# Nystrom attention with a gated MLP on one core: buffers at multiples of 64 bytes, one visit for W and its turned form, a shorter inverse root, another order in the first chunk

## The chip, the cores and the metric

One core of a Trainium2 chip runs the whole program. The metric is the device time of one execution in microseconds; it was measured three times before the change, and one more execution was profiled.

## What is computed

```python
def _attn_ref(q, k, v):                       # 8 batches, 8 heads, 576 tokens, 64 wide
    m = 32                                    # landmarks: means over 18 tokens
    scale = 1.0 / np.sqrt(D)
    ...
    A = sm(q, k_lm)                           # softmax of scaled products
    Bm = sm(q_lm, k_lm)
    C = sm(q_lm, k)
    Z = Bm.transpose(0, 1, 3, 2) / (norm1(Bm) * norminf(Bm) + 1e-06)
    for _ in range(6):
        Z = 2 * Z - Z @ Bm @ Z
    return (A @ Z @ C @ v).astype(np.float32)

def _moe_ref(x, w_gate, w_val, w_out, rms_g): # 4608 tokens of 512, d_ff 1536
    rms = np.sqrt(np.mean(x * x, axis=-1, keepdims=True) + 1e-06)
    xn = x / rms * rms_g
    g = xn @ w_gate
    silu = g * (1.0 / (1.0 + np.exp(-g)))
    val = xn @ w_val
    return (silu * val @ w_out).astype(np.float32)
```

The heads of the attention are joined to rows of 512, and these are the tokens of the MLP.

## The kernel before

**Stages of a batch.** `sums` makes the landmark sums lmT (DVE). `front` computes the products sC, sA and psB on PE, their maxima mx on DVE and the exponentials E on ACT; `turn` and `values` turn E and form C v (sE, ET, pCV); `soften` makes A. The inverse is a Newton iteration on PV: `newton_start`, six `newton_step`s (PE makes pn, DVE makes the next PV, the last one VF = 2 PV - pn). Then `newton_weights` multiplies with Bs into pW and copies it as W, and `newton_values` turns W on PE (pT) and multiplies with the gain gsb into WT. `second` computes the attention output pO from W and AT, its squares sq, their sums pss and pms, the inverse root of ms in r1 by operations on 18 columns (DVE), and an, AT scaled by the root, as a high part (ACT) and a low part (DVE).

**The MLP.** `mix_weights` multiplies WT with the gate and value weights of a pair of feature blocks, wgv, into pM, and splits it into Mhi and Mlo. So psg and psv come straight from an: per block and half of the tokens, 6 matmuls of 288 columns each for gate and value, in fp32r. SiLU is on ACT (s), the product with psv on DVE, and h holds the result's high and low part. Then pso sums h times the out weights (whio, wloo) over 6 blocks, 3 matmuls of 512 columns each, h stationary and the weights moving. d_ff is done in two halves: phase 1 goes over all batches with the first 6 blocks, phase 2 over all batches with the last 6 (lgv, lhio, lloo), and adds phase 1's sums. A chunk is one batch in one phase.

**Weights.** They are decoded from the bits read: two operations on ACT (L175, L178), two on DVE (L180, L183) for each quarter of a wgv, in the order of the class `Weights`.

**Order.** `Mixer` fills the MLP's matmuls with parts of later batches: each part is a generator that waits until a given number of matmuls of a chunk has been issued (`until`). For the first chunk these numbers are in the list `at` of `steady`, for the others in `enter` and `after`. `issue_after` holds an instruction behind another in the order. Each engine takes its instructions in the order of the program.

**Layout.** gsb takes 32 bytes of a partition, and with that the buffers allocated behind it (weights wgv, whio, wloo, an, s, h, Mhi, Mlo, qk, and lgv6 to lhio6 and lloo6) begin 32 bytes past a multiple of 64. lhio7 to lhio11 and lloo7 to lloo11, and the small pools on the other side, begin at multiples of 64.

## Time and profile before

| | |
|---|---|
| median of 3 runs | 837.14 us (836.75 to 837.6) |
| profiled execution | 836.84 us |
| its span in the trace | 834.7 us |
| PE busy | 800.4 us, 96% of the span |
| DVE, ACT, POOL busy | 490.9, 350.9, 71.0 us |
| chain that ended last | PE 86%, DVE 5%, DMA 4%, ACT 2% |
| PE in that chain | pso 35%, psg 19%, psv 18%, pM 6% |

The profiled execution is 0.3 us below the median, and 2.1 us of it lie around the span. A row of a timeline gives the start in us from the span's start, the duration, the engine, the line, and what is written from what. Matmul records overlap: the time of one in a row is the distance of two starts. An fp32 matmul stands as two records, an fp32r one as one.

### The profile page before, as it was taken

The page shows a single profiled execution, that of the slowest core. Times are in us where ns is not written, and L with a number is a line of the kernel's source. Part 1 is how long each engine was busy: PE and PEld are TensorE (multiplying, and loading weights), DVE is VectorE, ACT ScalarE, POOL GpSimd, SP SyncE. Part 2 cuts the span into 40 slices and gives each one's busy share as a digit, 9 for nine tenths or more (in the row PEclk, how much of TensorE's full clock was granted, in tenths as well). Part 3 has the DMA queues.
Part 4 walks back from the last instruction along what each step waited for, and adds up shares of the span by engine and source line. Part 5 has one row for each costly group of instructions (what it writes and reads, how often), then busy time and mean ns, then how long its engine had stood idle before and what let it go on. Part 6 is the DMA issues. An engine that isn't in the chain of part 4 may idle for free.

```text
span 834.7 us, 17401 instructions
## 1 busy us (share of the span) xinstructions
PE 800.4 (96%) x7192; PEld 630.3 (76%) x7192; DVE 490.9 (59%) x1095; ACT 350.9 (42%) x749; POOL 71.0 (9%) x97
## 2 busy tenths in 40 slices
PE   7756999999999999999999999999999999999998
PEld 4334667877878778777787879797979797979796
DVE  7787976856768748668584945242524252425241
ACT  4557644535445444445464844141414141414140
POOL 1012411020020200201110110000000000000000
PEclk8579999999999999999999999999999999999999
DMA  9756452250440612503436510413141304130202
GB/s 326 242 172 216 143 191 89 84 195 15 144 136 2 228 65 92 188 2 109 140 114 229 176 71 13 145 54 118 22 146 53 121 22 147 50 124 14 88 14 75
DMA packets 41054, 95.49 MB, mean 114 GB/s; under 512 B 4112, under 2 KB 17424, under 8 KB 38928
## 3 DMA queue, kind: packets, MB, share of 16 engines
q1 hardware_dynamic: 40976, 94.39, 33.4%
q8 instruction: 56, 0.92, 0.5%
q14 instruction: 22, 0.18, 0.1%
HBM read 66.06 MB, written 28.31 MB: 113 GB/s over the span
## 4 chain that ended last, share of the span: by engine, by line
PE 86%; DVE 5%; DMA 4%; ACT 2%; POOL 1%; issue 1%; SPq 1%; ACTq 0%; DVEq 0%
PE pso L109 35%; PE psg L109 19%; PE psv L109 18%; PE pM L109 6%; PE pn L109 2%; DMA wrawg<-in_moe_w_gate_dram 2%; PE pO L109 1%; PE sC L109 1%; PE pss L109 1%; DMA wrawv<-in_moe_w_val_dram 1%; PE pCV L109 1%; DMA qk<-in_k_dram 1%; PE sE L112 1%; DVE wgv L180 1%; SPq L152 0%
## 5 line engine op out<-in xcount | busy, mean ns | idle before, releaser
L109 PE MATMUL pso<-whio,h 128*128 128x512 f32 x432 | 140.7, 397 | 2.1 <-ACT ob L848 2.1
L109 PE MATMUL pso<-lhio,h 128*128 128x512 f32 x432 | 138.7, 396 | 0.0
L316 DVE TENSOR_TENSOR s<-s,psv 128x288 f32<-128x288 f32 x192 | 85.9, 450 | 60.0 <-PE psv L109 59.3
L315 ACT ACTIVATE s<-psg 128x288 f32<-128x288 f32 x192 | 78.7, 410 | 89.9 <-PE psg L109 89.5
L268 ACT CAST Mhi<-pM 128x512 fp32r<-128x512 f32 x96 | 51.4, 591 | 137.6 <-PE pM L109 137.2
L323 ACT CAST h<-s 128x576 fp32r<-128x576 f32 x96 | 64.6, 673 | 86.2 <-DVE s L316 86.2
L109 PEld LDWEIGHTS pso<-whio,h 128*128 128x128 f32 x432 | 81.6, 189 | 24.3 <-issue 4.2
L109 PEld LDWEIGHTS pso<-lhio,h 128*128 128x128 f32 x432 | 81.0, 187 | 24.8 <-DVE obl L911 5.9
L324 DVE TENSOR_TENSOR h<-s,h 128x576 fp32r<-128x576 f32 x96 | 72.7, 758 | 44.5 <-ACT h L323 44.3
L109 PE MATMUL psg<-an,Mhi 128*128 128x288 f32 x384 | 85.4, 307 | 4.8 <-ACT s L315 3.4
L911 DVE TENSOR_TENSOR obl<-obl,pso 128x512 f32<-128x512 f32 x36 | 24.8, 688 | 107.6 <-PE pso L109 107.4
L109 PE MATMUL pso<-wloo,h 128*128 128x512 f32 x216 | 86.4, 400 | 0.0
L109 PE MATMUL pso<-lloo,h 128*128 128x512 f32 x216 | 85.2, 395 | 0.0
L109 PE MATMUL psv<-an,Mhi 128*128 128x288 f32 x384 | 84.4, 303 | 0.0
L270 DVE TENSOR_TENSOR Mlo<-pM,Mhi 128x512 fp32r<-128x512 f32 x94 | 60.3, 683 | 37.5 <-ACT Mhi L268 37.5
L109 PE MATMUL psg<-anl,Mhi 128*128 128x288 f32 x384 | 81.7, 301 | 0.6 <-DVE Mlo L270 0.6
L109 PE MATMUL psv<-anl,Mhi 128*128 128x288 f32 x384 | 79.1, 294 | 0.0
L109 PEld LDWEIGHTS psg<-an,Mhi 128*128 128x128 f32 x384 | 62.3, 191 | 17.5 <-issue 6.7
L109 PEld LDWEIGHTS psg<-anl,Mhi 128*128 128x128 f32 x384 | 60.9, 188 | 15.5 <-issue 12.6
L109 PEld LDWEIGHTS psv<-an,Mhi 128*128 128x128 f32 x384 | 61.6, 188 | 6.1 <-issue 2.2
L109 PEld LDWEIGHTS psv<-anl,Mhi 128*128 128x128 f32 x384 | 61.5, 188 | 0.0
L109 PE MATMUL psg<-an,Mlo 128*128 128x288 f32 x192 | 58.5, 305 | 0.0
(138 smaller groups left out, 1249.8 us busy)
## 6 DMA issues: line engine op xcount, KB each, us to landing
qk<-in_q_dram SPq DMA_DIRECT2D x16, 576.0 KB, 4.8
qk<-in_k_dram SPq DMA_DIRECT2D x16, 576.0 KB, 5.8
ad<-an SPq DMA_DIRECT2D x8, 1152.0 KB, 5.1
pd<-ob SPq DMA_DIRECT2D x36, 256.0 KB, 2.4
anl<-ad SPq DMA_DIRECT2D x8, 1152.0 KB, 5.1
obl<-pd SPq DMA_DIRECT2D x36, 256.0 KB, 2.7
out_dram<-obl SPq DMA_DIRECT2D x36, 256.0 KB, 2.0
vt<-in_v_dram SPq DMA_DIRECT2D x16, 512.0 KB, 4.1
```

The costliest lines, as they stand in the source:

```text
L109: tc.keep_in_program_order(nc.tensor.matmul(*args, **kw))
L112: tc.keep_in_program_order(nc.tensor.transpose(*args))
L180: nc.vector.scalar_tensor_tensor(w, w, 3, wtail, op0=ALU.logical_shift_left, op1=ALU.bitwise_or)
L268: nc.scalar.copy(hi[:, g], ps[g])
L270: nc.vector.tensor_sub(lo[:, g], ps[g], hi[:, g].bitcast(F32))
L315: silu["last"] = nc.scalar.activation(s[:, cols], banks[0], AF.Silu).ins
L316: nc.vector.tensor_mul(s[:, cols], s[:, cols], banks[1])
L323: nc.scalar.copy(h[:, 0, TAIL:], s)
L324: gated[b, f0 // NF1, 2 * n + i] = nc.vector.tensor_sub(h[:, 1, TAIL:], s, h[:, 0, TAIL:].bitcast(F32))
L911: nc.vector.tensor_add(ob, ob, ps)
```

## The change

It has four parts. First, gsb is padded to 64 bytes and a new buffer `blocks` takes 1024, so that all the buffers named under Layout begin at multiples of 64. Second, `blocks` holds the four matrices Bs of a batch as a block diagonal (written by four POOL copies per batch); two matmuls with it give W's content and two more give it turned, both in one bank, so that the transposes of W and the copy between go, and the two functions become one; VF is written twice side by side for it. Third, the inverse root takes 8 operations on DVE where it took 10. Fourth, in the first chunk `sums(1, 0)` and `front(1, 0)` go between the parts of `second(0)`, ahead of the first `mix_weights`; the fifth quarter of the weights is decoded earlier; `sums(1, 1)` goes behind the decode of the second pair; the mix for the first chunk's next pair is taken one half later; and the positions of the later parts are other numbers (in the last list, that of the later batches, by one or a few).

```diff
     ones = cst.tile([P, M], F32, name="ones")
     nc.vector.memset(ones, 1.0)
-    gsb = cst.tile([P, NK], F32, name="gsb")
+    gsb = cst.tile([P, 16], F32, name="gsb")[:, :NK]
     WT = cst.tile([P, B, NK, 2 * M], F32, name="WT")
+    blocks = cst.tile([P, 2, P], F32, name="blocks")
+    nc.gpsimd.memset(blocks, 0.0)
...
-                if very and i and n + 1 < NPAIR:
-                    mix_weights(wts, b, pairs[n + 1])
-                    yield 1.1
                 s = mp.tile([P, S], F32, name="s", tag="s", bufs=2)
                 for e in range(2):
+                    if very and i and e and n + 1 < NPAIR:
+                        mix_weights(wts, b, pairs[n + 1])
+                        yield 1.1
                     cols = slice(e * HS, (e + 1) * HS)
                     banks = []
...
             if b:
-                tail(after)
+                tail(late or after)
...
             with tc.high_priority():
-                newton_weights(b, inverse[2])
-            yield 0.4, 0.0
-            yield from until(*next(at))
-            with tc.high_priority():
-                newton_values(b)
-            yield 0.3, 0.0
+                newton_weights(b)
+            yield 0.6, 0.0
             stage["newton"] = stage["wt"] = b
...
-            yield 0.0, TW
-            new_state(1)
-            sums(1, 0)
             while stage["second"] < 0:
                 yield -0.3
-            front(1, 0, fixed["an", 0].ins)
-            load_qk(2, 0)
-            yield 1.3, 0.0
-            sums(1, 1, fixed["mx", 1, 0].ins)
-            yield from until(0, 24)
+            yield from until(0, 12)
             turn(1, 0)
             yield 0.65, 0.0
-            yield from until(0, 36)
+            yield from until(0, 37)
+            sums(1, 1, early.last)
+            yield from until(0, 46)
             front(1, 1)
             load_qk(2, 1)
             yield 1.3, 0.0
             inverse = newton_start(1)
-            at = [46, 58, 70] + [78 + 8 * n for n in range(6)] + [126, 132, 138, n_gv + 4, n_gv + 10, n_gv + 18]
+            at = [54, 66, 78] + [84 + 7 * n for n in range(6)] + [126, 136, n_gv + 4, n_gv + 10, n_gv + 18]
             yield from rest(1, inverse, [(0, n) for n in at])
             for b in range(2, B):
...
-                after = [7 * n for n in range(7)] + [48, 54, 68, 86, 96]
+                after = [7 * n for n in range(6)] + [48, 56, 68, 86, 96]
                 yield from rest(b, inverse, [(c, n) for n in enter[3:]] + [(c + 1, n) for n in after])
...
+            Bs = sm.tile([P, 2, M], F32, name="Bs", tag="Bs", bufs=1)
             nc.vector.tensor_mul(Bs, Bm, den.unsqueeze(2).broadcast_to([P, 2, M]))
-            return BT, den, Bs
-
-        def newton_first(b, BT, den, Bs):
+            for h in range(4):
+                nc.gpsimd.tensor_copy(blocks[rows(h), :, rows(h ^ 1)], Bs[rows(h)])
+            return BT, den
+
+        def newton_first(b, BT, den):
             p0 = bmm(BT, BT, M, "p0")
...
                 pn = bmm(PV[:, :, :M], PV[:, :, M:], D, "pn")
-                nt["VF"] = to = sm.tile([P, 2, D], F32, name="VF", tag="VF", bufs=1)
-                of = PV[:, :, M:]
+                nt["VF"] = sm.tile([P, 2, 2, D], F32, name="VF", tag="VF", bufs=1)
+                for g in range(2):
+                    of, by = (a[:, g].unsqueeze(1).broadcast_to([P, 2, D]) for a in (PV[:, :, M:], pn))
+                    nc.vector.scalar_tensor_tensor(nt["VF"][:, g], of, 2.0, by, op0=ALU.mult, op1=ALU.subtract)
+                return
             nc.vector.scalar_tensor_tensor(to, of, 2.0, pn, op0=ALU.mult, op1=ALU.subtract)
 
-        def newton_weights(b, Bs):
+        def newton_weights(b):
+
             VF = state[b]["VF"]
-            pW = pa.tile([P, 2, D], F32, name="pW", tag="pa")
-            for g in range(2):
-                for h in range(4):
-                    r = rows(rho(g, h))
-                    mm(pW[rows(pos(g, h)), g], Bs[r, g, :], VF[r, g, :], start=True, stop=True)
-            W = sm.tile([P, 2, 2, D], F32, name="W", tag="W", bufs=2)
-            fixed[b] = nc.vector.tensor_copy(W, pW.unsqueeze(2).broadcast_to([P, 2, 2, D]))
+            pW = pa.tile([P, 2 * D + NK * 2 * M], F32, name="pW", tag="pa")
+            straight = pW[:, : 2 * D].rearrange("p (g d) -> p g d", g=2)
+            turned = pW[:, 2 * D :].rearrange("p (g n) -> p g n", g=2)
+            for g in range(2):
+                mm(straight[:, g], blocks[:, g], VF[:, g, 0], start=True, stop=True)
+            for g in range(2):
+                mm(turned[:, g], VF[:, g].rearrange("p a d -> p (a d)"), blocks[:, g], start=True, stop=True)
+            W = sm.tile([P, 2, D], F32, name="W", tag="W", bufs=2)
+            fixed[b] = nc.vector.tensor_copy(W, straight)
+            fixed["WT", b] = nc.vector.tensor_mul(
+                WT[:, b],
+                turned.rearrange("p g (j n) -> p (g j) n", j=2),
+                gsb.unsqueeze(2).broadcast_to([P, NK, 2 * M]),
+            )
             state[b]["W"] = W
-
-        def newton_values(b):
-            W = state[b]["W"]
-            pT = pa.tile([P, NK, 2 * M], F32, name="pT", tag="pa")
-            for g in range(2):
-                tp(
-                    pT[:, 2 * g : 2 * g + 2].rearrange("p j n -> p (j n)"),
-                    W[:, g].rearrange("p a d -> p (a d)"),
-                    ident,
-                )
-            nc.vector.tensor_mul(WT[:, b], pT, gsb.unsqueeze(2).broadcast_to([P, NK, 2 * M]))
 
         def newton(b):
...
                 yield 0.45, NP
-            newton_weights(b, inverse[2])
-            yield 0.4, WW
-            newton_values(b)
-            yield 0.3, WW
...
-            ri = r1.bitcast(I32)
-            nc.vector.tensor_single_scalar(ri, ms.bitcast(I32), 1, op=ALU.logical_shift_right)
-            nc.vector.tensor_scalar(ri, ri, -1, 0x5F3759DF, op0=ALU.mult, op1=ALU.add)
-            for c in (1.0, RS):
-                nc.vector.tensor_mul(r2, r1, r1)
-                nc.vector.scalar_tensor_tensor(r2, r2, c, ms, op0=ALU.mult, op1=ALU.mult)
-                nc.vector.scalar_tensor_tensor(r2, r2, -10.0 / 3.0, r2, op0=ALU.add, op1=ALU.mult)
-                last = nc.vector.scalar_tensor_tensor(r1, r2, 5.0, r1, op0=ALU.add, op1=ALU.mult)
+            nc.vector.tensor_scalar(
+                r1.bitcast(I32), ms.bitcast(I32), -0.5, 0x5F3759DF, op0=ALU.mult, op1=ALU.add
+            )
+            nc.vector.tensor_mul(r2, r1, r1)
+            nc.vector.scalar_tensor_tensor(r2, r2, -0.5, ms, op0=ALU.mult, op1=ALU.mult)
+            nc.vector.scalar_tensor_tensor(r1, r2, 1.5, r1, op0=ALU.add, op1=ALU.mult)
+            nc.vector.tensor_mul(r2, r1, r1)
+            nc.vector.tensor_mul(r2, r2, ms)
+            nc.vector.scalar_tensor_tensor(r2, r2, -10.0 / 3.0, r2, op0=ALU.add, op1=ALU.mult)
+            last = nc.vector.scalar_tensor_tensor(r1, r2, 5.0, r1, op0=ALU.add, op1=ALU.mult)
+            fixed["r1", b] = last
             if b == 0:
                 hold.enter_context(tc.issue_after(last.ins))
             an = mp.tile([P, 2, 2, S], F32R, name="an", tag="an", bufs=2)
-            rT = ap.tile([P, S], F32, name="rT", tag="rT", bufs=1)
+            rT = ap.tile([P, S], F32, name="rT", tag="sqT", bufs=1)
...
                 yield -0.3
-            for n, took in enumerate(second(0)):
-                yield took
-                if n == 2:
-                    low_parts = mix_weights(early, 0, 0, True)
-                    yield 1.1, 0.0
+            parts = second(0)
+            yield next(parts)
+            sums(1, 0, fixed[0].ins)
+            yield next(parts)
+            yield from parts
+            front(1, 0, fixed["r1", 0].ins, fixed["an", 0].ins)
+            load_qk(2, 0)
+            yield 1.3, 0.0
+            low_parts = mix_weights(early, 0, 0, True)
+            yield 1.1, 0.0
             low_parts()
             yield 0.5, 0.0
             stage["second"] = 0
 
         new_state(0)
...
+            while ("sums", 1) not in fixed:
+                yield -0.3
+            early.then = fixed["sums", 1].ins
+            yield from early.stream(WAIT0, 1)
 
         early.ahead, early.after = 2, fixed["eb", 0, 1].ins
         mix.add(first_second(), True)
```

**PE in the opening.** These are PE's instructions from batch 0's last Newton step to the first psg. Before:

```order
L109 MATMUL pn<-PV 32x64 x8
L109 MATMUL pW<-VF,Bs 32x64 x8
L112 MATMUL pT<-ident,W 128x128 x2
L109 MATMUL pO<-AT,W 64x288 x16
L109 MATMUL pss<-sq,ones 32x288 x8
L109 MATMUL pM<-wgv_417,WT 32x512 x8
L109 MATMUL pms<-sqT,sel 128x18
L109 MATMUL pM<-Mhi,minus 128x512 x2
L109 MATMUL sC<-qk_350,lmT 32x288
L109 MATMUL sA<-qk_350,lmT 32x288
```

After, up to the first two rows of front(1, 0), which reads qk_354:

```order
L111 MATMUL pn<-PV 32x64 x8
L111 MATMUL pW<-VF,blocks 128x64 x2
L111 MATMUL pW<-blocks,VF 128x128 x2
L111 MATMUL pO<-AT,W 64x288 x16
L111 MATMUL pss<-sq,ones 32x288 x8
L111 MATMUL pms<-sqT,sel 128x18
L111 MATMUL sC<-qk_354,lmT 32x288
L111 MATMUL sA<-qk_354,lmT 32x288
```

and behind the rest of that front:

```order
L111 MATMUL sA<-qk_354,lmT 32x288
L111 MATMUL sC<-lmT 32x32 x4
L111 MATMUL pM<-wgv_425,WT 32x512 x8
L111 MATMUL pM<-Mhi,minus 128x512 x2
L111 MATMUL psg<-an,Mhi 128x288 x2
L111 MATMUL psg<-an,Mlo 128x288
```

pW and pT have become two pairs of matmuls that follow each other; pM<-wgv and the pM that takes Mhi off have moved from between pss and sC to behind front(1, 0), and pms has moved ahead of both.

**DVE while the second pair is decoded.** wgv_664 before and wgv_554 after are the weights of pair 1; wgv_743 and wgv_755 those of pair 2; qk_353 and qk_357 belong to front(1, 1). Before, from that front's sums on:

```order
L380 TENSOR_REDUCE lmT<-qk_353 128x64 x2
L180 SCALAR_TENSOR_TENSOR wgv_664<-wgv_664,wrawg_356 128x4x128
L433 TENSOR_SCALAR ss<-ss 128x1
L434 TENSOR_SCALAR ss<-ss 128x1
L183 SCALAR_TENSOR_TENSOR wgv_664<-wrawg_356,wgv_664 128x4x128
L435 RECIPROCAL rs<-ss 128x2
L316 TENSOR_TENSOR s<-s,psv 128x288
L436 TENSOR_SCALAR Bm<-eb,rs 128x32
L180 SCALAR_TENSOR_TENSOR wgv_664<-wgv_664,wrawv_358 128x4x128
L316 TENSOR_TENSOR s<-s,psv 128x288
L183 SCALAR_TENSOR_TENSOR wgv_664<-wrawv_358,wgv_664 128x4x128
L180 SCALAR_TENSOR_TENSOR wgv_664<-wgv_664,wrawg_360 128x4x128
```

After, at the place where pair 1 is complete:

```order
L185 SCALAR_TENSOR_TENSOR wgv_554<-wrawv_362,wgv_554 128x4x128
L319 TENSOR_TENSOR s<-s,psv 128x288
L185 SCALAR_TENSOR_TENSOR wgv_554<-wrawg_364,wgv_554 128x4x128
L319 TENSOR_TENSOR s<-s,psv 128x288
L182 SCALAR_TENSOR_TENSOR wgv_554<-wgv_554,wrawv_366 128x4x128
L319 TENSOR_TENSOR s<-s,psv 128x288
L327 TENSOR_TENSOR h_713<-s,h_713 128x576
L185 SCALAR_TENSOR_TENSOR wgv_554<-wrawv_366,wgv_554 128x4x128
L182 SCALAR_TENSOR_TENSOR wgv_755<-wgv_755,wrawg_368 128x4x128
L185 SCALAR_TENSOR_TENSOR wgv_755<-wrawg_368,wgv_755 128x4x128
L383 TENSOR_REDUCE lmT<-qk_357 128x64 x2
L273 TENSOR_TENSOR Mlo<-pM,Mhi 128x512 x2
```

The sums of front(1, 1) stood ahead of all of pair 1's decode, and stand behind it and behind one quarter of pair 2. The first quarter of pair 1 is decoded still earlier, ahead of the sqT of batch 0, where pair 1 had none before.

**ACT around the second pair's Mhi.** Before:

```order
L323 CAST h_714<-s 128x576
L175 ACTIVATE wrawv_725<-wrawv_725 128x512
L178 ACTIVATE wgv_743<-wrawv_725 128x4x128
L175 ACTIVATE wrawg_748<-wrawg_748 128x512
L178 ACTIVATE wgv_743<-wrawg_748 128x4x128
L268 CAST Mhi<-pM 128x512 x2
L315 ACTIVATE s<-psg 128x288 x2
L424 ACT_TABLE_LOAD
```

After:

```order
L326 CAST h_713<-s 128x576
L177 ACTIVATE wrawv_725<-wrawv_725 128x512
L180 ACTIVATE wgv_755<-wrawv_725 128x4x128
L271 CAST Mhi<-pM 128x512 x2
L318 ACTIVATE s<-psg 128x288
L177 ACTIVATE wrawg_760<-wrawg_760 128x512
L180 ACTIVATE wgv_755<-wrawg_760 128x4x128
L427 ACT_TABLE_LOAD
```

The two operations on the weights of the second wrawg (wrawg_748 before, wrawg_760 after) stood ahead of Mhi and s, and stand behind them.

## Rows read from the trace of the kernel before

**Rows 1.** Busy time by window: stretch, its length, each engine, clock, DMA.

```profile
130.00:470.00 340.00, 339.15 (x3685) 263.68 (x3671) 238.99 (x586) 171.75 (x375) 31.25 (x40) 1.00 0.35 116
```

**Rows 2.** Waits of PE over the whole span, in total, times, longest.

```profile
PE pM L109 <- DVE wgv L183: 7.5, 1, 7.5
...
PE psg L109 <- ACT s L315: 3.4, 2, 2.9
PE pso L109 <- ACT ob L848: 2.1, 1, 2.1
```

**Rows 3.** Timeline of DVE in the opening: start us, us, operation [idle before].

```profile
38.71 0.48 DVE L748 STREAM_TRANSPOSE sqT<-pss 128x288 f32<-128x288 f32 x1 [0.50 <-PE pss L109]
...
41.30 0.18 DVE L759 TENSOR_SCALAR r<-ms 128x18 int32<-128x18 int32 x1
...
43.22 0.18 DVE L765 SCALAR_TENSOR_TENSOR r<-r,r 128x18 f32<-128x18 f32 x1
...
45.74 1.43 DVE L775 TENSOR_TENSOR an<-AT,an 128x576 fp32r<-128x576 f32 x2
...
48.88 2.57 DVE L380 TENSOR_REDUCE lmT<-qk 128x64 f32<-128x1152 f32 x2
...
57.97 0.68 DVE L183 SCALAR_TENSOR_TENSOR wgv<-wrawv,wgv 128x512 int32<-128x512 int32 x1
```

**Rows 4.** Timeline of ACT in the same stretch.

```profile
40.60 1.07 ACT L268 CAST Mhi<-pM 128x512 fp32r<-128x512 f32 x2 [3.31 <-PE pM L109]
...
48.22 1.28 ACT L424 ACT_TABLE_LOAD   x1
...
64.61 0.65 ACT L175 ACTIVATE wrawg<-wrawg 128x512 int32<-128x512 uint32 x1 [2.88 <-DMA wrawg<-in_moe_w_gate_dram]
```

**Rows 5.** Timeline of PE in the opening.

```profile
38.55 1.96 PE L109 MATMUL pM<-wgv,WT 64*32 64x512 f32 x16
40.44 0.61 PE L109 MATMUL pms<-sqT,sel 128*128 128x18 f32 x2
...
50.16 0.92 PE L112 MATMUL sE<-ident,E 128*128 128x128 f32 x4
```

**Rows 6.** Timeline of ACT around the end of the first chunk's MLP.

```profile
110.77 1.28 ACT L424 ACT_TABLE_LOAD   x1 [7.18 <-DVE mx L420]
...
112.56 1.23 ACT L774 CAST an<-AT 128x576 fp32r<-128x576 f32 x2
...
114.44 1.08 ACT L848 COPY ob<-pso 128x512 f32<-128x512 f32 x2
```

**Rows 7.** Timeline of PE around one later batch's pW and pT.

```profile
250.19 0.29 PE L109 MATMUL psg<-an,Mlo 128*128 128x288 f32 x1
250.41 0.42 PE L109 MATMUL pW<-VF,Bs 32*32 32x64 f32 x16
250.76 0.54 PE L109 MATMUL psv<-an,Mhi 128*128 128x288 f32 x2
...
251.68 0.38 PE L112 MATMUL pT<-ident,W 128*128 128x128 f32 x2
251.99 1.09 PE L109 MATMUL pM<-wgv,WT 64*32 64x512 f32 x16
```

**Rows 8.** Timeline of PE: pso of phase 1, first and last of 79.

```profile
478.10 0.39 PE L109 MATMUL pso<-wloo,h 128*128 128x512 f32 x1
...
495.78 0.39 PE L109 MATMUL pso<-wloo,h 128*128 128x512 f32 x1
```

**Rows 9.** Timeline of PE in phase 2: psg and psv, then pso.

```profile
600.13 0.30 PE L109 MATMUL psg<-anl,Mlo 128*128 128x288 f32 x1
...
602.91 0.30 PE L109 MATMUL psv<-anl,Mlo 128*128 128x288 f32 x1
...
603.97 0.39 PE L109 MATMUL pso<-lloo,h 128*128 128x512 f32 x1
...
610.95 0.40 PE L109 MATMUL pso<-lloo,h 128*128 128x512 f32 x1
```

More of the change, by code (lines that the diff above doesn't have):

```diff
@@ L130, in __init__ @@
             self.place = place
-            self.spots, self.ahead, self.after, self.then = spots, ahead, None, None
+            self.spots, self.ahead, self.after, self.then, self.last = spots, ahead, None, None, None
             self.raws, self.gv, self.out = {}, {}, {}
@@ L385, in sums, with front @@
                     )
-        def front(b, g, after=None):
+        def front(b, g, after=None, late=None):
             nt, lmT, qk = state[b], lms.pop((b, g)), loaded.pop((b, g))
@@ L706, in newton @@
                 yield 0.45, NP
[L707 to L710 removed]
+            newton_weights(b)
+            yield 0.6, WW
             stage["wt"] = b
@@ L814, in nystrom_moe_kernel @@
         new_state(0)
+        new_state(1)
         if WN0:
```

8 lines of the change are left out of this document (4 added, 4 removed).

## The prediction

> **What bounds the kernel now.** I read the table of windows first, then PE's waits, then the timelines of the stretches they point to. From 130 us on the kernel is bound by PE: 339.15 of 340 us busy at a granted clock of 1.00 [rows 1]. There a change counts only through what PE itself executes and at what rate. Before 130 us PE waits, and three single waits carry the worst of it: 7.5 us for the decode of the second pair's weights, 2.9 us for one SiLU, 2.1 us for a copy of pso [rows 2]. So I cost the edits in three lots: the opening, the end of the first chunk, and PE's rate.
>
> **The opening (first chunk, 38 to 80 us).** Before, pM(0,0) stands ahead of pms on PE: it starts at 38.55, takes 1.96, and pms starts at 40.44 [rows 5], though the second sqT was there at 38.71 + 0.48 = 39.19 [rows 3]. With pM behind front(1,0), pms follows sqT and ms, one step of 0.21 ahead of the root's first operation at 41.30 [rows 3], moves from 41.09 to about 40.05: -1.0. The ten operations of the inverse root run from 41.30 to 43.22 + 0.21, 0.213 each [rows 3]; eight take 1.70: -0.43. But the maxima of front(1,0) now lie between the root and an (two reduces, estimated at 0.4 each: lmT's two of 1152 columns take 2.57 [rows 3], and 288 are a quarter of one, with a fixed part), and ACT converts an's first half, then Mhi and Mlo, then the second half. Two Mhi casts take 1.07 [rows 4] and two Mlo casts are alike, so an's second half is ready at about 48.65, where before it was 45.74 + 1.43 = 47.17 [rows 3]. The first psg group is thus some 1.5 us later, not earlier.
>
> The gain comes after it. Pair 1's weights were complete at 57.97 + 0.68 = 58.65 [rows 3], behind lmT(1,1) (2.57 at 48.88) and behind the decodes of all its quarters [rows 3]. The order now decodes its first quarter before sqT (two operations gone from the queue, one every 0.6 or so at 0.68 a piece), puts lmT(1,1) behind pair 1 (-2.5), and one decode of pair 2 no longer cuts in (-0.6). With the 1.5 us of the later an: 58.65 - 1.2 - 2.5 - 0.6 + 1.5 = 55.85. PE has 36 psg/psv matmuls to do before it asks for these weights, where it had 24 and then the sE transposes at 50.16 [rows 5]; at 0.132 us each [rows 9] it runs dry at about 53.9. The wait of 7.5 [rows 2] becomes about 2.0; pM(0,1) is 2.7 earlier with 12 matmuls (1.6 us) more behind it: -4.3.
>
> The wait of 2.9 for a SiLU: ACT's queue held wrawg, which waited 2.88 for its DMA until 64.61 [rows 4], with Mhi and s behind it. In the new order Mhi and s stand ahead of that wrawg, so this wait goes: -2.9. Of the 7.2 I give back 2.2 until pM(0,2): lmT(1,1), moved behind the decodes, makes front(1,1) late; and although one change of ACT's table in the opening is saved (E comes directly, without the load at 48.22 and the one that leads back [rows 4]), front(1,1) and its turn now take two more pairs of loads at 1.28 a load, while SiLUs wait behind them. So -5.0 by pM(0,2); bounds -3.0 (both pairs, 5.1 us, reach PE but for about a fifth) and -6.5.
>
> **The end of the first chunk.** ACT waited until 110.77 for the maxima, then did a table load and an E before an (112.56, until 113.79), and another E before ob (114.44) [rows 6]; pso waited 2.1 for that ob [rows 2]. The new order puts an, an, ob, ob ahead of table and E. The load (1.28), the E ahead of an (0.5, what is left of 110.77 to 112.56) and the one behind it (0.65) leave ob's path; an still waits for AT: -1.3 (bounds 0 and -2.1). **The work of batch 1** between the two places now has its Newton steps 6 to 8 matmuls later, a second VF write and four POOL copies per batch, on a DVE and an ACT that the weights' decode still fills; no row prices what of this reaches PE. I take +1.8, with 0 and +4 (the size of one lost cover like the 2.9 plus a Newton step's wait) as bounds. Opening and first chunk together: -5.0 - 1.3 + 1.8 = -4.5.
>
> **W and its turned form in one visit.** Before, a batch paid psg 250.19 to psv 250.76 around pW, 0.57 where one step is 0.132, plus 0.13 in the next step, so 0.56; pT to pM took 251.99 - 251.68 = 0.31, some 0.22 more than going straight to pM [rows 7]. Together 0.78. Now there are four fp32 matmuls with a 128-column weight load, each of two records by the way the trace counts pW (16 records for 8 matmuls [rows 7]). The nearest row is pT, two records in 0.31 with the change to pM included, so 0.11 to 0.155 each: eight take 0.87 to 1.24, less 0.09 of changes counted twice: 0.78 to 1.15. Over the seven later batches that is 0 to +2.6 us; I take 0, because 0.11 is what follows without a change of operand. The wait W to pT falls away, but in these batches it was hidden behind psv matmuls. In batch 0 at half clock it was 1.2 us from pW to pT, and the eight records at half clock cost about as much: 0. The two operations less of the root, 0.43 a batch, lie beside PE's work [rows 1]: 0. Where psg and psv did not cover them, each batch would gain up to 0.43.
>
> **Buffers at multiples of 64 bytes.** This is the cost no row shows directly. The phases differ by it, though: pso's moving operand whio/wloo lies 32 bytes past a multiple of 64 as does h, its stationary one, while lhio7 to lhio11 and their low parts lie at a multiple and h does not. In phase 1, 78 pso matmuls (every third reads wloo) take 495.78 - 478.10 = 17.68, 226.7 ns each [rows 8]. In phase 2, 30 take 610.95 - 603.97 = 6.98, 232.7 ns each [rows 9]. Same columns, same engine, full clock. The reading that I take: what counts is whether the two operands lie alike. After the change all do, so the 540 pso matmuls of phase 2 on these buffers go to 226.7: -6.0 ns x 540 = -3.3 us. psg and psv (132.4 ns for 288 columns: 600.13 to 602.91 is 21 of them [rows 9]) lie alike before and after: 0. Bounds: nothing, and the two rivals below. A page of the Trainium skill speaks against this term: "SBUF — State Buffer", Specifications and Operand start alignment, gives lines of 16 bytes and asks only for a start at a multiple of the element size, adding that this is "about legality, not speed"; 32 and 64 are both multiples of 16, and by it the term would be 0 and the sum 3.3 higher. The trace's 226.7 against 232.7 is not explained by it.
>
> **The sum.** The profiled execution took 836.84 (a span of 834.7 and 2.1 around it), 0.3 below the median of the runs. 836.84 - 4.5 - 3.3 = 829.0; on the median's scale 829.3. A measurement of this kernel tells some 0.2%, 1.7 us, from no change.
>
> **Rivals.**
> *Alignment does nothing* (phase 2 is slower for another reason, such as the place in the memory): the opening alone, 837.1 - 4.5 = 832.6. For it: nothing but position separates the phases, and position has other sides than 64 bytes.
> *Every one of these matmuls gets cheaper.* At 2.4 GHz 512 columns are 213.3 ns and 288 are 120; phase 1 has 13.3 over that, psg 12.4 [rows 8, 9], and all of them read from 32 past a multiple. If 6 ns of it (the one step that the rows show) goes for all 3600: -21.6, with the opening and phase 2's own 3.3 -29.4: 808. Against it: the only aligned operand in the trace is in the slower phase. "TensorE: Matmul & The Clock Gate" in the Trainium skill (the section on back-to-back matmuls) states N/2.4 plus about 2.5 ns; by that floor the surplus of 10 to 17 ns over 3600 matmuls would be some 40 us, and the time about 793. No row of this case reaches that floor.
> *Slower: a moving operand at a multiple of 64 is the slow one*, wherever the stationary lies. Phase 2's rate fits that as well. Then the 648 pso of phase 1 and the 2304 psg and psv gain 6 ns each, +17.7, and phase 2 keeps its rate: 837.1 - 4.5 + 17.7 = 850; with pso alone 836.5. It decides from (4.5 + 1.7) / 2952 = 2.1 ns a matmul on.
> *The opening gives nothing net*: the later an, the late front(1,1) and the table loads eat the 7.2. Then 837.1 - 3.3 = 833.8. For it: three engines hand work to each other there, and DVE's queue ran without a pause to 58.65 [rows 3].
>
> **How the numbers follow.** My forecast 45% (829.3, by its own bounds 825 to 833), alignment without effect 15% (832.6), all cheaper 18% (808), slower 10% (836 to 850), opening eaten 12% (833.8). Range 813 to 836: it leaves out the lower half of the cheap case and most of the slow one. Faster by over 0.2% (below 835.5): all of the first and third, most of the second and fifth, 0.83. Slower (above 838.8): the slow case and a little of mixed mishaps, 0.10. Same: 0.07.
>
> **What would show each step.** pms within 0.3 us of the second sqT, eight root operations, and the first psg group later than before. The wait of pM on wgv near 2 us; the wait of 2.9 on s gone; two table loads around front(1,1), with SiLU behind them. ob at the chunk's end ahead of E. pso at 226.7 ns a matmul in both phases and psg at 132.4 as before; 220 in either phase means the cheap case, 232.7 in phase 1 the slow one. The visit of pW, eight records in 0.9 to 1.2 us. I would be wrong above all if the rate of 3600 matmuls moves, since 1 ns there is 3.6 us, more than most of the rest.

## The result and the profile after

The changed kernel took 829.62 us (median of 4 runs, 828.98 to 830.18); the kernel before, with one more run beside it, 836.94. The ratio is 0.9917 with a 95% interval of 0.9897 to 0.9937: faster by 0.6 to 1.0%. The forecast was 829.3. The profiled execution has a span of 827.2 us, 7.5 less than before. Where those 7.5 us lie, read from the start of PE's psg in three places:

| start on PE, us | before | after | difference | gained in the stretch |
|---|---|---|---|---|
| second chunk of phase 1, first psg | 131.72 | 126.68 | -5.04 | 5.04 |
| phase 2, first psg | 498.87 | 494.48 | -4.39 | -0.65 |
| phase 2, last pso | 830.68 | 823.17 | -7.51 | 3.12 |

The sum forecast for these was -4.5, 0 and -3.3. The total came out, and so did its three parts, nearly; inside the first part hardly a step did.

PE's waits over the whole span, the same view as [rows 2] (in total, times, longest):

```profile
...
PE sE L114 <- ACT E L427: 2.8, 3, 1.3
PE pCV L111 <- ACT ET L486: 2.6, 2, 2.0
PE pM L111 <- DVE wgv L185: 1.9, 1, 1.9
PE pO L111 <- ACT sq L733: 1.7, 2, 1.5
...
PE psg L111 <- ACT s L318: 1.6, 2, 1.1
...
PE pM L111 <- ACT Mhi L271: 1.2, 1, 1.2
...
```

The 7.5 for pair 1's weights has become 1.9, the longest for a SiLU 1.1 instead of 2.9, and the 2.1 of pso for ob has left the list. New are 1.5 for a square ahead of pO, and 1.2 for Mhi.

DVE in the opening, beside [rows 3]:

```profile
32.41 0.29 DVE L680 COPY W<-pW 128x128 f32<-128x128 f32 x1 [0.82 <-PE pW L111]
...
42.18 0.18 DVE L749 TENSOR_SCALAR ms<-pms 128x18 f32<-128x18 f32 x1 [0.71 <-PE pms L111]
...
49.86 0.76 DVE L772 TENSOR_TENSOR an<-AT,an 128x576 fp32r<-128x576 f32 x1 [2.07 <-ACT an L771]
...
57.56 0.45 DVE L319 TENSOR_TENSOR s<-s,psv 128x288 f32<-128x288 f32 x1 [0.52 <-PE psv L111]
57.94 0.75 DVE L327 TENSOR_TENSOR h<-s,h 128x576 fp32r<-128x576 f32 x1
58.61 0.69 DVE L185 SCALAR_TENSOR_TENSOR wgv<-wrawv,wgv 128x512 int32<-128x512 int32 x1
```

and PE there, beside [rows 5]:

```profile
30.33 1.08 PE L111 MATMUL pW<-VF,blocks 128*128 128x64 f32 x4 [0.50 <-DVE VF L665]
31.21 1.17 PE L111 MATMUL pW<-blocks,VF 128*128 128x128 f32 x4
...
35.56 1.54 PE L111 MATMUL pO<-AT,W 32*64 32x288 f32 x14 [1.55 <-ACT sq L733]
...
41.53 0.61 PE L111 MATMUL pms<-sqT,sel 128*128 128x18 f32 x2 [0.63 <-DVE sqT L742]
...
47.35 1.28 PE L111 MATMUL pM<-Mhi,minus 128*128 128x512 f32 x2 [1.18 <-ACT Mhi L271]
48.44 0.68 PE L111 MATMUL psg<-an,Mhi 128*128 128x288 f32 x2
```

The granted clock (the third number from the end) in the same stretch:

```profile
40.00:50.00 10.00, 7.73 (x72) 3.35 (x64) 6.44 (x21) 3.46 (x7) 0.00 (x0) 0.50 0.33 118
50.00:60.00 10.00, 7.93 (x54) 6.85 (x54) 7.99 (x18) 6.14 (x15) 0.62 (x1) 0.78 0.47 170
```

The opening begins later than before, not earlier. W is copied at 32.41, when all eight records of pW are through, though the first pair, which alone it reads, ends at 31.41. The squares of pO stand on ACT behind a weight that waits for its DMA, as the next rows show, so pO stops for 1.55. So pms starts at 41.53, 1.1 later than in [rows 5] instead of 1.2 earlier, and the second half of an is there at 49.86 + 0.76 = 50.62 instead of 47.17 [rows 3]. On ACT:

```profile
33.99 0.66 ACT L177 ACTIVATE wrawg<-wrawg 128x512 int32<-128x512 uint32 x1 [0.55 <-DMA wrawg<-in_moe_w_gate_dram]
34.56 0.65 ACT L180 ACTIVATE wgv<-wrawg 128x512 f32<-128x512 f32 x1
35.11 0.70 ACT L733 ACTIVATE sq<-pO 128x288 f32<-128x288 f32 x2
...
108.03 1.34 ACT L771 CAST an<-AT 128x576 fp32r<-128x576 f32 x2 [5.94 <-DVE AT L769]
109.28 1.07 ACT L855 COPY ob<-pso 128x512 f32<-128x512 f32 x2
110.37 1.28 ACT L427 ACT_TABLE_LOAD   x1
```

The last three rows answer to [rows 6]: an and ob now stand ahead of the table load, and PE does not wait for ob. One visit of a later batch, beside [rows 7]:

```profile
246.17 0.29 PE L111 MATMUL psv<-an,Mlo 128*128 128x288 f32 x1
246.30 0.55 PE L111 MATMUL pW<-VF,blocks 128*128 128x64 f32 x4
246.69 0.66 PE L111 MATMUL pW<-blocks,VF 128*128 128x128 f32 x4
247.28 1.09 PE L111 MATMUL pM<-wgv,WT 64*32 64x512 f32 x16
```

Eight records take 247.28 - 246.30 = 0.98. And pso in both phases, beside [rows 8, 9]:

```profile
473.71 0.39 PE L111 MATMUL pso<-wloo,h 128*128 128x512 f32 x1
...
491.39 0.39 PE L111 MATMUL pso<-wloo,h 128*128 128x512 f32 x1
```

```profile
599.41 0.39 PE L111 MATMUL pso<-lloo,h 128*128 128x512 f32 x1
...
605.53 0.39 PE L111 MATMUL pso<-lloo,h 128*128 128x512 f32 x1
```

The 78 of phase 1 take 17.68 us as before, 226.7 each; 27 of phase 2 take 6.12, 226.7 each, where they took 232.7.

### The profile page after: what moved, and what is told of

Read it like the earlier page. It is cut to its first block, busy times and chain, and to the rows that moved or that the text cites. A ratio compares the mean times of both kernels' runs of the same rounds, so it can differ in the third digit from the quotient of the medians.

```text
span 827.2 us, 17286 instructions
## 1 busy us (share of the span) xinstructions
PE 796.6 (96%) x7112; PEld 634.8 (77%) x7112; DVE 490.8 (59%) x1087; ACT 351.1 (42%) x749; POOL 78.7 (10%) x130
## 4 chain that ended last, share of the span: by engine, by line
PE 86%; DVE 6%; DMA 3%; ACT 2%; issue 1%; SPq 1%; POOL 1%; DVEq 0%; ACTq 0%
PE pso L111 34%; PE psg L111 19%; PE psv L111 18%; PE pM L111 5%; DMA wrawg<-in_moe_w_gate_dram 2%; PE pn L111 2%; PE sC L111 1%; PE pO L111 1%; PE pss L111 1%; PE pCV L111 1%; DMA qk<-in_k_dram 1%; PE sE L114 1%; SPq L154 1%; PE pW L111 1%; DVE h L327 0%
## 5 line engine op out<-in xcount | busy, mean ns | idle before, releaser
L111 PE MATMUL pso<-lhio,h 128*128 128x512 f32 x432 | 136.5, 392 | 0.0
L327 DVE TENSOR_TENSOR h<-s,h 128x576 fp32r<-128x576 f32 x96 | 74.4, 775 | 42.0 <-ACT h L326 41.6
L111 PE MATMUL psv<-an,Mlo 128*128 128x288 f32 x192 | 59.0, 307 | 0.0
```

The costliest lines, as they stand in the source:

```text
L111: tc.keep_in_program_order(nc.tensor.matmul(*args, **kw))
L327: gated[b, f0 // NF1, 2 * n + i] = nc.vector.tensor_sub(h[:, 1, TAIL:], s, h[:, 0, TAIL:].bitcast(F32))
```

## The experiments

Two measures are used. The ratio to the kernel before comes from runs in rounds, and its interval is some 0.3% wide. The starts of PE's psg in the profile are finer: chunk by chunk they repeat to 0.02 us from 131 us on, but the opening varies from one execution to the next, perhaps by 1 us, as the first experiment will show; whole runs of one kernel spread wider (the five of the old opening from 830.06 to 833.15, the profiled one at 833.11). The table gives the differences to the profile of before at the places of the first table, in us.

| kernel | median, us | ratio (95%) | second chunk | phase 2 | last pso |
|---|---|---|---|---|---|
| the change | 829.62 | 0.9917 (0.9897 to 0.9937) | -5.04 | -4.39 | -7.51 |
| pad alone | 832.87 | 0.9958 (0.9941 to 0.9975) | -1.21 | -1.16 | -4.64 |
| change without pad | 832.22 | 0.9948 (0.9934 to 0.9963) | -5.25 | -4.64 | -4.30 |
| out weights off by 32 and 64 | 833.97, one run | | -4.21 | -1.32 | -2.54 |
| out weights off by 16 and 4 | 834.03, one run | | -6.08 | -3.87 | -2.46 |
| old opening | 832.81 | 0.9954 (0.9940 to 0.9968) | -0.90 | -0.22 | -3.38 |
| sums back | 833.49 | 0.9969 (0.9958 to 0.9979) | +0.01 | +0.70 | -2.77 |
| W first | 834.95 | 0.9988 (0.9979 to 0.9997) | -2.12 | +2.45 | -0.68 |
| two visits | 827.93 | 0.9906 (0.9892 to 0.9921) | -5.05 | -5.02 | -8.51 |
| long root | 829.70 | 0.9923 (0.9906 to 0.9940) | -4.61 | -3.94 | -7.45 |
| two visits, first mix early | 826.57 | 0.9885 (0.9870 to 0.9901) | -7.52 | -7.48 | -10.97 |
| two visits, decode ahead | 830.10 | 0.9927 (0.9912 to 0.9942) | -3.16 | -3.16 | -6.66 |
| two visits, first mix early, last decode | 826.34 | 0.9879 (0.9861 to 0.9897) | -6.88 | -6.80 | -10.30 |

In phase 2 one step of 0.36 us, ahead of the last chunk's pso, is there in some executions (the change, change without pad, W first, and others) and missing in others; differences at the last pso are known to no better than that.

**Pad alone.** To the kernel before:

```diff
-    gsb = cst.tile([P, NK], F32, name="gsb")
+    gsb = cst.tile([P, 16], F32, name="gsb")[:, :NK]
```

> The kernel before with gsb padded to 64 bytes and nothing else, so that every operand of psg, psv and pso lies at a multiple of 64. Theory (what counts is whether the two operands of a matmul lie alike): pso of phase 2 falls from 232.7 to 226.7 ns a matmul, phase 1, psg and psv stay; the time falls by 3 to 3.5 us, to about 833.6. Rival (phase 2 became faster through something else in the change, such as the shifted weights' order or less DVE work there): phase 2 stays at 232.7 and the time at 837. Second rival (a side effect of the new positions in the opening): the opening moves too, by more than 0.5 us.

Phase 2 takes 4.64 - 1.16 = 3.48 us less, in steps of 0.38 or 0.49 a chunk, the very steps of the changed kernel. The median duration of lhio's rows falls with it to whio's (the three numbers are the least, the median and the greatest, ns). Before:

```profile
L109 PE MATMUL pso<-lhio,h x432: 387/394/501, 519.5 to 830.7; 128*128 128x512 f32 x144
```

With the pad:

```profile
L109 PE MATMUL pso<-whio,h x432: 387/389/628, 95.8 to 494.9; 128*128 128x512 f32 x144
...
L109 PE MATMUL pso<-lhio,h x432: 387/389/496, 518.3 to 826.0; 128*128 128x512 f32 x144
```

So 32 bytes of padding are worth the whole of the second term. The opening moved by 1.2 us in the profile, more than the 0.5 that the second rival had as its mark. But the ratio is 0.42%, 3.5 us, which phase 2 accounts for alone, so I take the 1.2 for the spread between executions; the runs of before themselves lie between 834.67 and 837.78. That padding also helps the opening is not excluded.

**Change without pad.** The same line, undone in the changed kernel.

> The changed kernel without the padding of gsb; blocks and all the rest stay, and h and whio go back to 32 bytes past a multiple of 64, lhio7 to lhio11 stay at a multiple. Theory: phase 2 goes back to 232.7 ns a matmul, phase 1 keeps 226.7, and the time rises by 3 to 3.5 us to about 832.9. Rival (position in the memory, since blocks still shifts everything by 1024 bytes): no change, 829.6.

From the first psg of phase 2 to the last pso the difference to before stays but for that step of 0.36 (-4.64 to -4.30), so phase 2 runs at its old rate. Its place in the memory is still 1024 bytes further on, so place is not the cause.

**Out weights off by 32 and 64, and by 16 and 4 bytes.** The moving operands of pso, inside larger tiles:

```diff
-            return [wp.tile([P, DM], F32R, ...) for t in ("hi", "lo")]
+            return [wp.tile([P, DM + 32], F32R, ...)[:, 8 : 8 + DM] for t in ("hi", "lo")]
...
-                pool.tile([P, DM], F32R, ...) for t in ("hi", "lo")
+                pool.tile([P, DM + 32], F32R, ...)[:, 16 : 16 + DM] for t in ("hi", "lo")
```

> The changed kernel with the moving weights of pso shifted inside larger buffers, h unmoved at a multiple of 64: whio and wloo by 32 bytes (phase 1: moving off, stationary on, the reverse of phase 2 before), lhio and lloo by 64 bytes. Theory (alike in 64 bytes or not): phase 1 rises to about 232.7 ns a matmul, phase 2 stays at 226.7, the time rises by some 3.5 us. Rival A (only a moving operand on a multiple with a stationary one off it is slow): phase 1 stays at 226.7. Rival B (alike must mean in 128 bytes): phase 2 rises too, 7 us in all.

The second has 4 and 1 elements in place of 8 and 16. A tile of DM + 32 elements takes 2176 bytes, 17 times 128, where it took 2048; so each low part also lies 128 bytes further against its high part than in the changed kernel, and the distances hold modulo 128 alone.

> As the one before it, with whio and wloo shifted by 16 bytes and lhio and lloo by 4 bytes against h. Theory in its strict form (any difference within 64 bytes): both phases rise to 230 ns or more, the time by 5 to 8 us. Rival (only the half of 64 bytes counts, or full 16-byte pieces): a shift of 16 costs in phase 1 and one of 4 in phase 2 nothing, or neither costs anything.

With the first, whio in phase 1 has the median that lhio has before:

```profile
L111 PE MATMUL pso<-whio,h x432: 387/394/506, 95.9 to 494.7; 128*128 128x512 f32 x144
```

The mean distance of two pso starts, over the 517 pairs of phase 1 and 626 of phase 2 from 131 us on that follow each other within 300 ns, worked out from the traces:

| kernel | phase 1: moving against stationary | ns | phase 2 | ns |
|---|---|---|---|---|
| before | equal (both 32 past) | 228.3 | 32 apart, but for lhio6 | 232.8 |
| the change | equal | 228.3 | equal | 227.4 |
| off by 32 and 64 | 32 apart | 232.7 | 64 apart | 230.6 |
| off by 16 and 4 | 16 apart | 231.1 | 4 apart | 234.6 |

(The equal case is 226.7 in an uninterrupted run; the mean has the first matmuls of each run in it.) The reverse of phase 2's old state, moving off and stationary on a multiple, runs at the same mean as that state (232.7 and 232.8; over the equal state of the same phase that is 4.4 and 5.4 ns, and in the old state one block of six was alike): the rival that made only one of the two the slow one is refuted, unless the 128 bytes of the low parts alone make phase 1 slow, which no run separates. So is the one that needs 16 bytes or half of 64: 4 bytes cost most. 64 bytes apart cost 3.2 ns against the 5.4 of 32 in the same phase, so equal to 64 bytes is not enough. In the changed kernel, and with the pad alone, the buffers are placed so that h and all of whio, wloo, lhio and lloo are equal to 256 bytes; 128 bytes apart were not tried by themselves, so whether 128 is enough is open.

One thing does not fit the simplest form of the reading. In phase 2 of before, lhio6 and lloo6 lie like h, yet their matmuls are 231.5 apart on the mean, hardly less than those of lhio7 behind them (231.7); lhio8 to lhio11 have 233.3. In the changed kernel these are 228.4, 228.1 and 227.0. What one equal block gains may be spread over it and the next, or the pair of operands is not all that counts; no run separates the two.

**Old opening.** The changed kernel with these places as before:

```diff
...
+            front(1, 0, fixed["an", 0].ins)
+            load_qk(2, 0)
+            yield 1.3, 0.0
+            sums(1, 1, fixed["mx", 1, 0].ins)
+            yield from until(0, 24)
             turn(1, 0)
...
-            parts = second(0)
-            yield next(parts)
-            sums(1, 0, fixed[0].ins)
...
-            front(1, 0, fixed["r1", 0].ins, fixed["an", 0].ins)
...
+            for n, took in enumerate(second(0)):
+                yield took
+                if n == 2:
+                    low_parts = mix_weights(early, 0, 0, True)
...
```

> The changed kernel with the order of the first chunk as before (places of sums(1, 0), front(1, 0), the first mixes, turn(1, 0), sums(1, 1), front(1, 1), the fifth quarter's decode and batch 1's Newton steps), with the padding, the one visit and the short root kept. Theory (the order of the opening is worth 4.5 us): the wait for pair 1's weights is 7 us again, the one for a SiLU 2.9, the one for ob 2.1; phase 2 stays at 226.7 ns; about 833.5. Rival (the opening's gain comes from the shorter root and the one visit): 830.5 or less.

The order is worth 5.04 - 0.90 = 4.1 us in the profile and, by the ratios, 0.9954 less 0.9917, 3.1. The wait for pair 1's weights is 6.5 again, that for a SiLU only 1.4. The wait of pso for ob has not come back, so this part is not the order's.

**Sums back.** One call moved in the changed kernel:

```diff
             while stage["second"] < 0:
                 yield -0.3
+            sums(1, 1, fixed["mx", 1, 0].ins)
             yield from until(0, 12)
             turn(1, 0)
             yield 0.65, 0.0
             yield from until(0, 37)
-            sums(1, 1, early.last)
```

> The changed kernel with sums(1, 1) alone moved back to directly behind front(1, 0), ahead of pair 1's decode. Theory (those 2.5 us of DVE are what pair 1 waited for): the wait of pM on the weights grows from 1.9 to about 4.4, front(1, 1) does not wait any more (0.7 less); 1 to 2 us slower, about 831.1. Rival (the 2.5 us only change place, since front(1, 1) is then early and batch 1's chain goes on sooner): within 0.5 us of 829.6.

It costs 4 to 5 us, all of the opening's gain and more than twice what was expected, and by another way. DVE around an, and PE's waits between 40 and 130 us:

```profile
48.27 2.60 DVE L383 TENSOR_REDUCE lmT<-qk 128x64 f32<-128x1152 f32 x2
50.79 0.75 DVE L772 TENSOR_TENSOR an<-AT,an 128x576 fp32r<-128x576 f32 x1
```

```profile
PE sE L114 <- ACT E L427: 3.2, 2, 2.1
PE psg L111 <- ACT s L318: 2.9, 1, 2.9
PE psv L111 <- DVE s L319: 2.0, 1, 2.0
PE pM L111 <- DVE wgv L185: 1.9, 1, 1.9
PE psg L111 <- DVE Mlo L273: 1.3, 1, 1.3
```

lmT falls into the time in which DVE waits for ACT's half of an, so it delays an by only 0.9 (50.79 against 49.86), and the wait for pair 1's weights is 1.9 as without it. What grows is behind: batch 1's front comes at another place in the queues of ACT and DVE, and sE, a SiLU, an s and an Mlo are late by 1.3 to 2.9 each.

**W first.** The copy of W written ahead of the turned matmuls:

```diff
             for g in range(2):
                 mm(straight[:, g], blocks[:, g], VF[:, g, 0], start=True, stop=True)
+            W = sm.tile([P, 2, D], F32, name="W", tag="W", bufs=2)
+            fixed[b] = nc.vector.tensor_copy(W, straight)
             for g in range(2):
                 mm(turned[:, g], VF[:, g].rearrange("p a d -> p (a d)"), blocks[:, g], start=True, stop=True)
-            W = sm.tile([P, 2, D], F32, name="W", tag="W", bufs=2)
-            fixed[b] = nc.vector.tensor_copy(W, straight)
```

> The changed kernel with the copy of W written ahead of the two turned matmuls, so that it waits for the first pair alone. In the trace of the changed kernel W is copied at 32.41, after all eight records, though the first pair ends at 31.4. Theory: W is there 1.0 us earlier, pO and all behind it to the first psg follow, and 0.5 to 1.0 us remain at the end: about 828.8. Rival (ACT, which holds the squares of pO behind a weight's arrival until 35.1, and the later waits take it up): 829.6 within 0.3.

It does not answer its question. The program now makes the turned matmuls wait for the copy, since both are in one tile, and PE pays that in every batch (40 to 470 us):

```profile
PE pW L111 <- DVE W L678: 3.7, 7, 1.1
```

The first psg is 0.9 us earlier than in the changed kernel (47.56 against 48.44), and phase 1 loses 4.6 us where the changed kernel loses 0.65. With two tiles in place of one it was not tried.

**Two visits.** The changed kernel with `newton_weights` and `newton_values` of before, W of double width, VF written once and no POOL copies; the position lists have the one entry more that this takes.

```diff
-                newton_weights(b)
-            yield 0.6, 0.0
+                newton_weights(b)
+            yield 0.4, 0.0
+            yield from until(*next(at))
+            with tc.high_priority():
+                newton_values(b)
+            yield 0.3, 0.0
```

> The changed kernel with the two visits of before (eight matmuls of 32 x 64 into pW, W twice as wide, two transposes into pT, WT from these), without blocks' POOL copies and the second VF; padding, root and the new order kept, the added position in the lists halfway between its neighbours. Theory (one visit is neutral on PE but for 0.11 us a batch that it costs from the second to the seventh): the chunks of phase 1 each lose 0.11 us of the visit's excess, 0.7 in all, and batch 0 has W about 1 us earlier; 828.2 to 829. Rival (one visit saves a wait that the traces hide behind psv): slower by 0.5 to 2 us.

The 0.65 us that the changed kernel gives back from chunk to chunk in phase 1 are gone (-5.05 to -5.02), and at the second chunk the two are equal (-5.05 and -5.04), though W is copied at 31.24 instead of 32.41 and the first psg starts 1.1 us earlier. So the one visit costs PE 0.11 us a batch and gains nothing in the first chunk. By the ratios the difference, 0.9917 to 0.9906, is within the intervals; the steps of the trace carry this verdict.

**Long root.** The ten operations of before in the changed kernel.

```diff
...
+            for c in (1.0, RS):
+                nc.vector.tensor_mul(r2, r1, r1)
+                nc.vector.scalar_tensor_tensor(r2, r2, c, ms, op0=ALU.mult, op1=ALU.mult)
+                nc.vector.scalar_tensor_tensor(r2, r2, -10.0 / 3.0, r2, op0=ALU.add, op1=ALU.mult)
+                last = nc.vector.scalar_tensor_tensor(r1, r2, 5.0, r1, op0=ALU.add, op1=ALU.mult)
...
```

> The changed kernel with the inverse root of before, ten operations instead of eight. Theory (the two operations, 0.43 us, lie on the path in batch 0 only and beside PE's work in all later batches): the first psg 0.4 us later, the later chunks unchanged to 0.05, 0.2 to 0.5 us slower, about 830.0. Rival (each batch pays 0.43): 833.

At the second chunk it is 0.43 us behind the changed kernel, and every later step is the same, so no later batch pays for the root. The times cannot tell them apart. But the first chunk's end is as in [rows 6] again, on ACT:

```profile
107.70 1.28 ACT L427 ACT_TABLE_LOAD   x1 [5.72 <-DVE mx L423]
...
109.49 1.23 ACT L769 CAST an<-AT 128x576 fp32r<-128x576 f32 x2
...
111.38 1.07 ACT L853 COPY ob<-pso 128x512 f32<-128x512 f32 x2
```

and pso waits 2.1 for ob (109.94 to 112.02 on PE). It is the shorter root, not the new order, that put an and ob ahead of the table load; with the old opening and the short root they stand ahead of it too.

**Two visits, first mix early.** To the kernel with two visits:

```diff
             yield next(parts)
-            yield from parts
-            front(1, 0, fixed["r1", 0].ins, fixed["an", 0].ins)
-            load_qk(2, 0)
-            yield 1.3, 0.0
+            yield next(parts)
             low_parts = mix_weights(early, 0, 0, True)
             yield 1.1, 0.0
+            yield from parts
+            front(1, 0, fixed["r1", 0].ins, fixed["an", 0].ins)
+            load_qk(2, 0)
+            yield 1.3, 0.0
```

> The kernel with two visits (padding, short root and new order kept) with the first pM back ahead of pms, as before the change, and front(1, 0) still ahead of psg. In the changed kernel pM waits behind front(1, 0), its Mhi comes between the halves of an on ACT, PE idles 1.2 us for Mhi and its clock is granted in full only at 53.8, where before it was at 44.7. Theory (the move of the first pM is what made the first psg 2.7 us later): pms 1.3 us later, but an's halves follow each other, the first psg is whole 1 to 1.5 us earlier, and the time falls by 0.5 to 1.5 us to about 827. Rival (pair 1's weights and the waits behind them take it up): 828 within 0.3.

2.5 us less at the second chunk than with two visits alone, kept to the end: 826.57, below both kernels. Its PE from the first pM on:

```profile
40.14 1.38 PE L111 MATMUL pM<-wgv,WT 64*32 64x512 f32 x16
41.44 0.40 PE L111 MATMUL pms<-sqT,sel 128*128 128x18 f32 x2
42.95 0.74 PE L111 MATMUL pM<-Mhi,minus 128*128 128x512 f32 x2
46.56 0.40 PE L111 MATMUL psg<-an,Mhi 128*128 128x288 f32 x1 [2.87 <-ACT an L776]
```

pM follows pss without a pause and takes 1.38 where it took 1.96 in [rows 5]: PE's clock has risen in it. The granted clock from 40 to 50 us is 0.84, with two visits alone 0.67, in the changed kernel 0.50 (there it is full from some 54.4 us on, by its 0.78 from 50 to 60 us, not from the 53.8 of the expectation). So pms comes no later than in the changed kernel (41.44 against 41.53), Mhi and Mlo are made before an asks for ACT, and the halves of an follow each other: the second is done at 47.97 (46.54 and 1.43 for both), where with two visits alone it was 49.52. What of this is the clock's and what ACT's order was not separated.

**Two visits, decode ahead.** Pair 1's last decode forced ahead of the first h, by asking for pair 1 there and holding the low part of h behind it.

```diff
+                first = very and not n and not i
+                if first:
+                    wts.get("gv", pairs[1])
...
-                gated[b, f0 // NF1, 2 * n + i] = nc.vector.tensor_sub(...)
+                with tc.issue_after(wts.last) if first else nullcontext():
+                    gated[b, f0 // NF1, 2 * n + i] = nc.vector.tensor_sub(...)
```

> The kernel with two visits (padding, short root and new order kept) with pair 1's last decode ahead of the low part of the first h on DVE; in the changed kernel it stands behind that h and the third s, which wait for PE and ACT, and ends at 59.3. Theory (the place of that one decode is what is left of the wait for pair 1, not lmT): the wait of pM on wgv falls from 1.9 to below 0.8, and 0.5 to 1.2 us remain at the end: about 827. Rival (the decodes of pair 2 that come forward with it hold ACT's queue for their DMA, with a SiLU behind them): a new wait of 2 us or more near 64, and 828 or slower.

Both halves of the expectation came: the wait on the weights falls to 0.8, so that decode's place is what was left of it, and the rival's new wait arrives with it, because pair 2's decodes came forward too:

```profile
PE sC L111 <- DMA wrawv<-in_moe_w_val_dram: 3.1, 1, 3.1
...
```

In sum 1.9 us worse at the second chunk than two visits.

**Two visits, first mix early, last decode.** As the two before together, with the stream of decodes skipping the turn that was taken ahead (`wts.skip`), so that pair 2's stay where they were.

> The kernel with two visits and the first pM ahead of pms, and pair 1's last decode ahead of the low part of the first h on DVE without bringing pair 2's decodes forward; with it the fourth SiLU comes ahead of front(1, 1)'s exponentials on ACT, and two table loads (2.6 us) go. Theory (after the first psg, what remains in this stretch are queues: one decode's place and ACT's tables): the wait of pM on wgv falls from 1.9 to about 1.2, the wait of 0.9 on s goes, and the time falls by 0.7 to 2 us to about 825.3. Rival (the order of E behind the fourth SiLU holds batch 1's chain, and its waits grow by as much): 826.6 within 0.5, or slower.

The wait on the weights falls from 1.9 to 1.2 and two table loads go, but front(1, 1) on PE is now late by 0.7 and 1.8 and batch 1's first Newton step by 2.2. At the second chunk it is 0.6 us behind the kernel with the early mix; its median of 826.34 is the same within the intervals. The rival is right.

## Why the prediction was right

**The second term, buffers alike.** Right in mechanism and size: -3.3 forecast, 3.1 in the trace of the change (3.5 but for that step of 0.36) and 3.5 with the pad alone, phase 2 at 226.7 ns a matmul, phase 1 unmoved, psg and psv unmoved (132.6 and 132.5 on the mean, before and after). The forecast's 6.0 ns over 540 matmuls is a little small because the 30 matmuls of its 232.7 have three of lhio6 among them; the means of the whole phase, 232.8 and 227.4 over 648, give the 3.5. The reading taken, that the two operands' places against each other count, is borne out by padding alone, by taking the padding out and by the reversed distance; how lhio6 fits, and to how many bytes the places must be equal, stay open. The rivals of no effect, of everything cheaper and of a slow multiple of 64 all fall with the pad alone and with the weights off by 32. Of the rule in "SBUF — State Buffer" in the Trainium skill it has to be said that it speaks of legality: here both operands kept to it, and the rate of the matmul still depends on their addresses.

**The first term, the opening and the first chunk.** -4.5 forecast, -5.0 in the profile (4.1 of it the order by the profile of the old opening, 3.1 by the ratios). The sum is right, its three parts are not. PE at pM(0,1), pM(0,2) and the first pso, before and after:

```profile
58.71 1.96 PE L109 MATMUL pM<-wgv,WT 64*32 64x512 f32 x16 [7.52 <-DVE wgv L183]
...
78.73 2.29 PE L109 MATMUL pM<-wgv,WT 64*32 64x512 f32 x16 [1.81 <-DVE nden L648]
...
97.05 0.40 PE L109 MATMUL pso<-whio,h 128*128 128x512 f32 x1
```

```profile
59.35 1.09 PE L111 MATMUL pM<-wgv,WT 64*32 64x512 f32 x16 [1.89 <-DVE wgv L185]
...
78.71 1.96 PE L111 MATMUL pM<-wgv,WT 64*32 64x512 f32 x16
...
95.10 0.40 PE L111 MATMUL pso<-whio,h 128*128 128x512 f32 x1
```

At pM(0,2) the changed kernel is level with the one before with 12 psg and psv matmuls more behind it: 1.6 ahead, where 5.0 were forecast with 3.0 as the least. Inside this the 2.9 for the SiLU (3.0) and the 2.2 given back (2.4) came out; the 4.3 at pM(0,1) did not, it is 0.9: that pM starts 0.6 later than before and not 2.7 earlier, with the same 12 matmuls more done.

At the first pso it is 2.0 ahead, so the 1.8 for batch 1's work is not given back. From there to the second chunk it gains another 3.1, where 1.3 were forecast with 2.1 as the most. In this last stretch the granted clock is 1.00 in the changed kernel and 0.95 before, where it falls behind the wait for ob (0.83 from 110 to 120 us); the prediction has no term for that. With the long root the wait for ob is there, the clock stays at 1.00, and the stretch takes 32.1 us, against 31.6 in the changed kernel and 34.7 before; PE is busy for 28.7 of it, against 29.1 and 31.8, with the same number of instructions to within one. So most of the 3.1 goes with the clock and not with the wait, as far as kernels that differ in more than this can show it.

Four steps of the path failed:
- "pms follows sqT and ms moves from 41.09 to about 40.05": ms is at 42.18. I took the eight records and the two visits as equal in batch 0 without asking which of them W's copy waits for, and I overlooked ACT: the squares stand behind a weight that has not landed. With the two visits back, W is 1.2 us earlier and ms still at 41.37: the two transposes of sqT come at 39.20 and 40.18, later than in [rows 3].
- The first psg "some 1.5 us later": its start is 2.7 later, and PE's clock is at half, 1.2 GHz, through the whole of 40 to 50 us, where the profile of before has 0.75. I did not ask what new pauses on PE (0.63 ahead of pms, 1.18 ahead of the second pM) would do to the clock. The experiment with the early mix fills these two, leaves one of 2.9 ahead of psg, and gives 2.5 us back.
- "lmT(1,1) behind pair 1 (-2.5)" in pair 1's queue: the wait did fall to the 2.0 forecast (1.9), but not for that, and some 3.5 us later than forecast. Pair 1's last decode stands behind s and h, which wait for PE, with lmT in either place; the experiments with the sums back and with the decode ahead show it. The place of lmT is worth more than I gave it, 4 to 5 us, but in the queues behind front(1, 1).
- "The new order puts an, an, ob, ob ahead of table and E: -1.3": the wait of 2.1 went, 1.1 for E is there in its place; the shorter root is what did it, which I had costed at nothing there, and with the long root the second chunk starts only 0.43 later.

That the three parts add up to the forecast is luck: the opening fell short by 3.4 us, and the parts behind it made up 2.1 and 1.8.

**The visit.** Costed at 0 of 0 to +2.6 us, it measures 0.11 us a batch, 0.65 in all: a record takes 0.12 (0.98 for eight), not the 0.11 that I chose at the low end of the row's bounds. A mis-sized term, in the range.

**The root.** Nothing in the later batches, as forecast; 0.4 in the opening and the first chunk.

## What to carry to other kernels

Where a tuned stream of matmuls runs at two rates with the same shape, look early at the byte addresses of both operands against each other: one padded tile of 64 bytes was worth 3.5 us of 837 here, nearly half of a change of many lines. In an opening where four engines hand work round, a moved instruction should be followed to the engines' queues behind it, not only to the wait that it was meant for: both edits at the one wait that was left shifted it to other places. And a piece of PE's work put into a pause ahead of a critical chain need not delay the chain: here it came through at a higher granted clock.

## What was not expected of the hardware

A matmul of 128x128 by 512 columns in fp32r takes 226.7 ns where its two SBUF operands lie equal to 256 bytes, and 3 to 7 ns more on the mean of a phase where they are 4, 16, 32 or 64 bytes apart, counted modulo 128; 4 bytes cost most (234.6), and 64 less than 32 (230.6 against 232.7). The matmuls of 288 columns take 132.5 in all these kernels; their operands are alike in each, and were not set apart.
